# The bias of ScalarE's exps: a constant in the instruction instead of a column in on-chip memory

## The chip, the cores and the metric

The kernel runs on one core of a Trainium2 chip. The metric is the time of one execution on the device, in microseconds (us). The core has a matmul engine (TensorE, PE in the profile; PEld is its weight loads), three engines that work on elements (VectorE is DVE, ScalarE is ACT, GpSimd is POOL) and a queue that only issues DMAs (SyncE, SP). Each works through its own list of instructions in order, and waits on semaphores for the others.

## The reference

Two attention blocks are computed from inputs of their own, and their outputs stand side by side. Each has 2048 rows of 640 numbers in bfloat16, 32 heads of 20.

```python
# A: softmax attention
qkv = (x @ wqkv) -> q, k, v          # 32 heads, 2048 x 20 each
scores = q @ k^T * 20 ** -0.5        # 2048 x 2048 per head
a = (softmax(scores) @ v) @ wo
# B: linear attention
phi(t) = where(t > 0, t + 1, exp(t)) + 1e-6
kv, z = phi(k)^T @ v, sum over s of phi(k)
b = ((phi(q) @ kv) / (phi(q) . z + 1e-6)) @ wo
out = concatenate([a, b])            # 2048 x 1280
```

The large part is block A: 32 heads x 2048 x 2048 scores, each of which needs an exponential.

## The kernel before

**Tiles of A.** A stage `n` is one group of four heads and one block of 512 queries; there are 8 x 4 = 32 of them. Keys are taken 128 at a time. One score matmul (`score`) makes the scores of one head, 128 keys and 512 queries, in one bank of PSUM, the memory into which TensorE writes. It uses 20 rows of the array, so that up to four heads run beside one another. Scores stand with keys on the partitions and queries along the row. The weighted sum of V (`pv_quad`) takes the exponentials as they are; a column of ones in V gives the denominator, by which the result is divided once a stage is complete (`norm`). So a factor that is common to all exponentials drops out.

**Exponentials in two ways.** Most tiles go to ScalarE: `emit_exp` makes one ACTIVATE of a group of three or two tiles in turn (banks 0 to 2, or banks 3 and 4), 1536 or 1024 numbers on each of 128 partitions, and writes bfloat16 into the ring `f_PT`. It computes exp(scale x score + bias), with scale 20 ** -0.5 and bias (42 + 0.000108) ln 2: the factor 2 ** 42 is that of the other way, so that both are on one scale. One or two of the 16 blocks of keys in each stage but one (`ND`) go to VectorE, which forms the exponential in integer and polynomial steps (`d_score`: L1286 once for each tile, then L1297, L1301 and L1305 for two tiles at once) and writes it into `f_PD`.

**The bias column.** `alloc` reserves `f_eb`, 128 partitions of one float32. GpSimd fills it at the start (L1035, in `start_loads`), and each exp of L1251 is given a pointer to it. Block B's exps (`phi`, L1554: 320 or 512 numbers, out of PSUM, into float32) have no bias argument, so the instruction holds the constant 0, and scale 1.

**The loop.** `run` goes over the groups `j`. In each round it writes, for TensorE, the scores of group `j + 1` (`emit_scores`), for ScalarE the exp of group `j`, and then for TensorE products with V and work of the background: projections of Q, K and V, all of block B, and the output projections, whose results VectorE, ScalarE and GpSimd carry on. Scores of group `j + 1` go into the banks that the exp of group `j - 1` reads, so they wait until it is done. Everything else on TensorE that stands ahead of them in its list delays them as well.

**What sets the order.** The lists are written when the kernel is built, by a planner (`_Sched`, `_Clock`) that keeps an assumed time for each engine. It takes 0.062 + 0.4267 n us for an exp of n tiles (L1254) and fills TensorE up to the assumed end of that exp. Where TensorE would have too little to do, it adds matmuls of zeros (`zeros` and `fill`, operands `f_g` and `f_z`) until its sum of assumed work within 3.41 us is at least `FLOOR` = 1.45. `_Sched` writes a wait only where no earlier wait of the engine covers it. At the end a value is read that decides whether a general form of block A is run as well; with these inputs it is not.

Of the kernel before, what the change touches and what calls it, by code (L numbers as in the profile page):

```python
# [5 lines left out]
F32 = mybir.dt.float32  # L6
# [718 lines left out]
LN2 = 0.6931471805599453  # L725
# [74 lines left out]
class _Fast:  # L800
# [53 lines left out]
    def alloc(self):  # L854
        S, NT = self.S, self.NT
        self.KT = self.sb("f_KT", [128, 2, S], BF16)
        self.Qr = self.sb("f_Qr", [128, 4, 512], BF16)
        self.V = self.sb("f_V", [128, NT, N_HEADS, 21], BF16)
        self.xT = self.sb("f_xT", [128, N_DC, S], BF16)
        self.wA = self.sb("f_wA", [128, N_DC, 3 * D_MODEL], BF16)  # L860
        self.wo = self.wA[:, :, 2 * D_MODEL:3 * D_MODEL]
        self.wo7 = self.sb("f_wo7", [128, D_MODEL], BF16)
        self.PT = self.sb("f_PT", [128, self.NPT, 512], BF16)
        self.PD = self.sb("f_PD", [128, self.NPD, 512], BF16)
        self.W = self.sb("f_W", [128, 2, 1024], F32)
        self.PL = self.sb("f_PL", [128, 2, 1024], F32)
        self.T1 = self.sb("f_T1", [128, 512], F32)
        self.Tn = self.sb("f_Tn", [128, 512], BF16)
        self.OTp = self.sb("f_OTp", [128, 512], BF16)
        self.R = self.sb("f_R", [128, 32], F32)  # L870
        self.OTd = self.sb("f_OTd", [128, N_DC, S], BF16)
        self.stage = self.sb("f_st", [128, 4, D_MODEL], BF16)
        self.wBq = self.sb("f_wBq", [128, N_DC, D_MODEL], BF16)
        self.wBkv = self.sb("f_wBkv", [128, N_DC, 2 * D_MODEL], BF16)
        self.woB = self.wBkv[:, :, 0:D_MODEL]
        self.pqT = self.wBkv[:, :, D_MODEL:D_MODEL + 512]
        self.xBt = self.sb("f_xB", [128, 2, N_DC, 512], BF16)
        self.xB = [self.xBt[:, k] for k in range(2)]
        self.kvm = self.sb("f_kvm", [128, N_DC, 21 * N_HEADS], BF16)
        self.kvx = self.sb("f_kvx", [128, 2688 + 10 * 168 + 5 * 168], BF16)  # L880
        self.va = self.kvx[:, 0:2688].rearrange("p (t h j) -> p t h j", t=4, j=21)
        self.kvacc = self.kvx[:, 2688:4368].bitcast(F32).rearrange("p (c n) -> p c n", c=N_DC)
        self.mask = self.kvx[:, 4368:5208].rearrange("p (c n) -> p c n", c=N_DC)
        self.part = self.kvx[:, 0:5120].bitcast(F32).rearrange("p (k n) -> p k n", k=8)
        self.pko = self.sb("f_pk", [128, 4 * D_MODEL], BF16)
        self.pk = self.pko[:].rearrange("p (t n) -> p t n", t=4)
        self.o = self.pko[:, 0:2 * D_MODEL].rearrange("p (t n) -> p t n", t=2)
        self.oT = self.pko[:, 2 * D_MODEL:4 * D_MODEL].rearrange("p (t c m) -> p t c m", t=2, c=N_DC)
        self.ex = self.sb("f_ex", [128, 2, 512], F32)
        self.r1 = self.sb("f_r1", [128, 2, 512], F32)  # L890
        self.rd = self.sb("f_rd", [128, 2, 2, 16], F32)
        self.Z = self.sb("f_z", [128, 128], BF16)
        self.G = self.sb("f_g", [128, 128], BF16)
        self.ebias = self.sb("f_eb", [128, 1], F32)
        self.gmx = self.sb("f_gmx", [128, 2], F32)
        self.ident = self.sb("f_id", [128, 128], BF16)
        self.flag = self.sb("f_flag", [128, 1], I32)
        self.bmx = self.sb("f_bmx", [128, 1], F32)
        self.warm = self.sb("f_warm", [128, 1], F32)
        self.ones = self.sb("f_ones", [128, 1], F32)  # L900
# [115 lines left out]
    def start_loads(self):  # L1016
        sch = self.sch
        awq = self.Aw.rearrange("(c p) n -> p c n", p=128)
        x2 = self.Ax[0]
        xn = self.stage  # L1020
        M = D_MODEL
        for k in range(2):
            sch.dma("sp", lambda e, k=k: e.dma_start(
                xn[:, 2 * k:2 * k + 2, :], x2[256 * k:256 * (k + 1), :].rearrange("(t p) d -> p t d", p=128)),
                writes=tuple(("xn", t) for t in (2 * k, 2 * k + 1)), cost=(0.1, 3.5))
        parts = ((0, 92, ("wq", 0)), (M, M + 92, ("wk", 0)), (2 * M, 2 * M + 160, ("wv", 0)),
                 (M + 92, 2 * M, ("wk", 1)), (92, M, ("wq", 1)), (2 * M + 160, 3 * M, ("wv", 1)))

        def load(q, part):
            a, b, res = part  # L1030
            sch.dma(q, lambda e: e.dma_start(self.wA[:, :, a:b], awq[:, :, a:b]), writes=(res,),
                    cost=(0.5, 5.0 if b - a < 200 else 8.0))
        sch.op("dve", lambda e: e.memset(self.warm[:], 0.0), writes=("warm",))
        sch.op("dve", lambda e: e.memset(self.OTp[:], 1.0), writes=("OTp",), cost=0.3)
        sch.op("pool", lambda e: e.memset(self.ebias[:], (self.OCT + self.EXP_S) * LN2), writes=("ebias",), cost=0.1)  # L1035
        sch.op("act", lambda e: e.activation(self.warm[:], self.warm[:], AF.Exp), writes=("warm",), cost=1.5)
        load("act", parts[0])
        load("act", parts[1])
        load("sp", parts[2])
        for tc in range(1, self.NQC):  # L1040
            for c in range(N_DC):
                sch.dma("sp", lambda e, c=c, tc=tc: e.dma_start_transpose(
                    self.xT[:, c, 512 * tc:512 * (tc + 1)], x2[512 * tc:512 * (tc + 1), 128 * c:128 * (c + 1)]),
                    writes=(("xT", c, tc),), cost=(1.65, 2.0))
        for part in parts[3:]:
            load("sp", part)
# [195 lines left out]
    def emit_exp(self, j):  # L1242
        sch, ps = self.sch, self.ps
        grp = self.groups[j]
        b0 = self.SB[j % 2][0]
        u0 = self.ustart[j]
        s0 = u0 % self.NPT
        n = len(grp)
        assert u0 + n - 1 - self.NPT < 4 * self.pvnext
        scale = float(D_HEAD) ** -0.5  # L1250
        sch.op("act", lambda e: e.activation(self.PT[:, s0:s0 + n, :], ps[:, b0:b0 + n, :], AF.Exp,  # L1251
                                             bias=self.ebias[:, 0:1], scale=scale),
               reads=tuple(("ps", b0 + k) for k in range(n)) + ("ebias",),
               writes=tuple(("PT", s0 + k) for k in range(n)), cost=0.062 + 0.4267 * n)  # L1254

    def d_ready(self, slack):
# [773 lines left out]
```

## Time and profile before

| | us |
|---|---|
| median of 3 runs | 960.22 (959.16 to 965.89) |
| the profiled execution | 961.13 |
| its span, first to last instruction | 959.0 |
| ScalarE busy | 928.6 |
| TensorE busy | 778.2 |
| VectorE busy | 722.0 |
| GpSimd busy | 160.5 |

A row of the groups gives the source line, the engine, the operation, `out<-in` by the names of the tiles, the shapes, the count; then the busy time and the mean duration of one in ns; then how long the engine had been idle just before them, and what ended that. L179 is a helper through which nearly all matmuls are issued, so they are told apart by their operands: `f_Qr,f_KT` are scores, `f_PT,f_V` and `f_PD,f_V` products with V, `f_xT,f_wA` projections of A, `f_wBkv`, `f_xB` and `f_wBq` block B, `f_g,f_z` zeros. The row of clock digits in the slices is the share of its full clock that TensorE was granted, in tenths. In the chain of work each piece has its start, its length and the number of its instructions. In a table of windows each stretch has its length, the busy time and count of each engine (or of one line alone), the granted clock, the share of the DMA engines and GB/s.

### The profile page before, as it was taken

Reading aid. Unit: us, or ns where it says so; the run is one execution under the profiler, and the core shown is the slowest. Engines: PE = TensorE matmul, PEld = TensorE weight load, DVE = VectorE, ACT = ScalarE, POOL = GpSimd, SP = SyncE. Lnnn points to the kernel's source line nnn. Section 1 sums busy time; section 2 is a strip of 40 time slices with the busy share of each in tenths; the row PEclk is TensorE's granted clock in tenths of the full one; section 3 lists DMA queues with packets and bytes.
Section 4 is the critical chain, followed back from the end, with each engine's and each line's share of the span. In section 5 each row is a group of like instructions: output and inputs, shape, how many; then the busy total and the mean of one; then the engine's idle time right before and its main releaser. Section 6 shows DMA issues by size and latency. Waiting matters only on the chain.

```text
span 959.0 us, 24384 instructions
## 1 busy us (share of the span) xinstructions
PE 778.2 (81%) x10963; PEld 244.7 (26%) x10963; DVE 722.0 (75%) x1003; ACT 928.6 (97%) x799; POOL 160.5 (17%) x154
## 2 busy tenths in 40 slices
PE   8877788777778787877788877778887888889986
PEld 3322222222222222322232222212221222223332
DVE  6769576784678888887868787878787788877475
ACT  6999999999999999999989999999999999999996
POOL 3012200010131223221103300041004103200000
PEclk9999979999998999999988899999999999999999
DMA  6900000000001000100040000010001000000001
GB/s 127 251 5 5 4 15 19 4 5 5 16 28 29 5 5 5 32 5 1 5 69 4 2 4 12 19 39 3 21 15 32 12 19 12 1 12 26 33 32 59
DMA packets 45742, 23.93 MB, mean 25 GB/s; under 512 B 33984, under 2 KB 44992, under 8 KB 45632
## 3 DMA queue, kind: packets, MB, share of 16 engines
q1 hardware_dynamic: 44176, 21.92, 9.8%
q8 instruction: 87, 1.43, 0.6%
q10 hardware_dynamic: 1456, 0.40, 0.2%
q14 instruction: 23, 0.19, 0.1%
HBM read 7.31 MB, written 5.24 MB: 13 GB/s over the span
## 4 chain that ended last, share of the span: by engine, by line
ACT 84%; PE 12%; issue 1%; DVE 1%; POOL 0%; DMA 0%; SPq 0%; ACTq 0%
ACT f_PT L1251 81%; PE ps L179 12%; ACT f_ex L1554 2%; DMA f_OTd<-f_OTp 0%; DVE f_PL L1297 0%; SPq L1428 0%; POOL f_pk L1559 0%; PE ps L1064 0%; POOL f_Tn L1409 0%; DVE f_OTp L1416 0%; ACT f_st L1528 0%; DVE f_PD L1305 0%; DVE f_PL L1301 0%; DVE f_kvx L1465 0%; DVE f_V L1178 0%
## 5 line engine op out<-in xcount | busy, mean ns | idle before, releaser
L1251 ACT ACTIVATE f_PT<-ps,f_eb 128x1536 bf16<-128x1536 f32 x739 | 918.3, 1527 | 14.5 <-PE ps L179 14.2
L179 PE MATMUL ps<-f_Qr,f_KT 20*128 20x512 bf16 x2048 | 320.0, 395 | 166.7 <-ACT f_PT L1251 150.8
L179 PE MATMUL ps<-f_g,f_z 32*128 32x512 bf16 (+3 forms) x857 | 227.4, 396 | 0.0
L1286 DVE TENSOR_SCALAR f_W<-ps 128x512 f32<-128x512 f32 x200 | 138.2, 691 | 117.0 <-PE ps L179 113.3
L179 PEld LDWEIGHTS ps<-f_Qr,f_KT 20*128 20x128 bf16 x2048 | 77.7, 91 | 456.6 <-ACT f_PT L1251 425.6
L179 PE MATMUL ps<-f_PT,f_V 128*21 128x512 bf16 x1848 | 189.0, 399 | 1.0 <-ACT f_PT L1251 1.0
L1305 DVE SCALAR_TENSOR_TENSOR f_PD<-f_PL,f_W 128x1024 uint16<-128x1024 f32 x100 | 126.6, 1266 | 0.7
L1301 DVE SCALAR_TENSOR_TENSOR f_PL<-f_W,f_PL 128x1024 f32<-128x1024 uint16 x100 | 126.1, 1262 | 0.9
L1297 DVE SCALAR_TENSOR_TENSOR f_PL<-f_W 128x1024 f32<-128x1024 uint16 x100 | 126.3, 1267 | 0.4
L1409 POOL TENSOR_TENSOR f_Tn<-f_T,f_R 128x320 bf16<-128x320 f32 x31 | 39.2, 1264 | 432.4 <-DVE f_R L1406 432.4
L179 PE MATMUL ps<-f_xT,f_wA 128*32 128x512 bf16 x1280 | 107.4, 406 | 0.0
L1557 POOL TENSOR_SCALAR f_ex<-f_ex 128x320 f32<-128x320 f32 (+1 forms) x52 | 41.3, 795 | 328.1 <-ACT f_ex L1554 328.1
L179 PEld LDWEIGHTS ps<-f_PT,f_V 128*21 128x21 bf16 x1848 | 45.4, 89 | 111.6 <-issue 109.3
L179 PE MATMUL ps<-f_wBkv,f_xB 128*32 128x320 bf16 x1280 | 69.2, 304 | 0.0
L179 PEld LDWEIGHTS ps<-f_g,f_z 32*128 32x128 bf16 (+1 forms) x857 | 53.3, 92 | 7.9 <-issue 7.0
L1559 POOL TENSOR_TENSOR f_pk<-f_ex,f_r 128x320 bf16<-128x320 f32 x32 | 38.4, 1201 | 2.7
L179 PEld LDWEIGHTS ps<-f_xT,f_wA 128*32 128x32 bf16 x1280 | 30.0, 97 | 29.6 <-issue 18.2
L1550 DVE TENSOR_SCALAR f_r<-ps 128x320 f32<-128x320 f32 (+1 forms) x52 | 29.2, 561 | 10.6 <-PE ps L179 10.1
L1554 ACT ACTIVATE f_ex<-ps 128x320 f32<-128x320 f32 (+1 forms) x52 | 36.7, 706 | 0.1
L179 PEld LDWEIGHTS ps<-f_wBkv,f_xB 128*32 128x32 bf16 x1280 | 30.3, 96 | 21.1 <-issue 11.0
L179 PE MATMUL ps<-f_xB,f_wBq 128*32 128x512 bf16 x400 | 34.8, 418 | 0.0
L1399 DVE STREAM_TRANSPOSE f_T<-ps 128x512 f32<-128x512 f32 x32 | 22.8, 713 | 15.7 <-PE ps L179 15.6
(80 smaller groups left out, 504.5 us busy)
## 6 DMA issues: line engine op xcount, KB each, us to landing
out_dram<-f_st SPq DMA_DIRECT2D x31, 160.0 KB
f_OTd<-f_OTp SPq DMA_DIRECT2D x108, 20.0 KB
f_wBkv<-in_B_wqkv_dram SPq DMA_DIRECT2D x1, 1600.0 KB
f_wA<-in_A_wqkv_dram SPq DMA_DIRECT2D x2, 685.0 KB
f_wBq<-in_B_wqkv_dram SPq DMA_DIRECT2D x1, 800.0 KB
f_wA<-in_A_wo_dram SPq DMA_DIRECT2D x1, 800.0 KB
f_wBkv<-in_B_wo_dram SPq DMA_DIRECT2D x1, 800.0 KB
f_st<-in_A_x_dram SPq DMA_DIRECT2D x2, 320.0 KB
```

What stands on the lines that cost most here:

```text
L179: lambda e: e.matmul(out, lhsT, rhs, start=start, stop=stop, tile_position=tp, skip_group_check=sgc),
L1251: sch.op("act", lambda e: e.activation(self.PT[:, s0:s0 + n, :], ps[:, b0:b0 + n, :], AF.Exp, bias=self.ebias[:, 0:1], scale=scale), reads ...
L1286: self.dve(0.69, lambda e: e.tensor_scalar(dst, ps[:, b, :], cs, cb, op0=ALU.mult, op1=ALU.add), reads=(("ps", b),), writes=(("W", x, h),))
L1297: self.dve(1.29, lambda e: e.scalar_tensor_tensor(pl, lo, self.EXP_A, lo, op0=ALU.add, op1=ALU.mult), reads=rw, writes=(("PL", x),), fill= ...
L1301: self.dve(1.29, lambda e: e.scalar_tensor_tensor(pl, lo, self.EXP_B, pl, op0=ALU.add, op1=ALU.mult), reads=rw, writes=(("PL", x),), fill= ...
L1305: self.dve(1.29, lambda e: e.scalar_tensor_tensor(pd, pl, self.EXP_K, w, op0=ALU.mult, op1=ALU.add), reads=rw + (("PL", x),), writes=(("PD ...
L1399: self.dve(0.69, lambda e: e.transpose(T1[:], ps[:, self.PVB, :]), reads=(("ps", self.PVB),), writes=("T1",))
L1409: sch.op("pool", lambda e: e.tensor_tensor(n3[:, :, 0:D_HEAD], t3[:, :, 0:D_HEAD], rb, op=ALU.mult), reads=("T1", ("R", n % 2)), writes=(" ...
L1550: self.dve(0.16 + 0.00104 * n, lambda e: e.tensor_scalar(r1, src, 0.0, 1e-6, op0=ALU.max, op1=ALU.add), reads=(("ps", b),), writes=(("r1", ...
L1554: sch.op("act", lambda e: e.activation(ex, src, AF.Exp), reads=(("ps", b),), writes=(("ex", k),), cost=0.05 + 0.00084 * n)
L1557: sch.op("pool", lambda e: e.tensor_scalar(ex, ex, 1.0, 0.0, op0=ALU.min, op1=ALU.max), writes=(("ex", k),), cost=0.1 + 0.0019 * n)
L1559: self.done[key] = sch.op("pool", lambda e: e.tensor_tensor(dst, ex, r1, op=ALU.add), reads=(("ex", k), ("r1", k)), writes=(res,), cost=0. ...
```

## The change

The column and the instruction that fills it are left out, and the exps are given the number itself. It is the same number in float32. The built instruction of L1251 then has a constant as its bias operand, where it had an address.

```diff
@@ alloc
-        self.ebias = self.sb("f_eb", [128, 1], F32)
@@ start_loads
-        sch.op("pool", lambda e: e.memset(self.ebias[:], (self.OCT + self.EXP_S) * LN2), writes=("ebias",), cost=0.1)
@@ emit_exp
         sch.op("act", lambda e: e.activation(self.PT[:, s0:s0 + n, :], ps[:, b0:b0 + n, :], AF.Exp,
-                                             bias=self.ebias[:, 0:1], scale=scale),
-               reads=tuple(("ps", b0 + k) for k in range(n)) + ("ebias",),
+                                             bias=(self.OCT + self.EXP_S) * LN2, scale=scale),
+               reads=tuple(("ps", b0 + k) for k in range(n)),
                writes=tuple(("PT", s0 + k) for k in range(n)), cost=0.062 + 0.4267 * n)
```

## The prediction

> **What bounds the kernel now.** I read the page's parts 1 and 4 first, for the engine on which the end hangs.
>
> ```profile
> span 959.0 us, 24384 instructions
> PE 778.2 (81%) x10963; PEld 244.7 (26%) x10963; DVE 722.0 (75%) x1003; ACT 928.6 (97%) x799; POOL 160.5 (17%) x154
> PEclk9999979999998999999988899999999999999999
> ACT f_PT L1251 81%; PE ps L179 12%; ACT f_ex L1554 2%; DMA f_OTd<-f_OTp 0%; DVE f_PL L1297 0%; SPq L1428 0%; POOL f_pk L1559 0%; PE ps L1064 0%; POOL f_Tn L1409 0%; DVE f_OTp L1416 0%; ACT f_st L1528 0%; DVE f_PD L1305 0%; DVE f_PL L1301 0%; DVE f_kvx L1465 0%; DVE f_V L1178 0%
> L1251 ACT ACTIVATE f_PT<-ps,f_eb 128x1536 bf16<-128x1536 f32 x739 | 918.3, 1527 | 14.5 <-PE ps L179 14.2
> ```
>
> ScalarE is busy 97% of the span, 918.3 us of it with 739 exps of one line, L1251, and that line holds 81% of the chain that ended last. It stood idle for matmuls 14.2 us in all. The operands say `f_PT<-ps,f_eb`: each of these exps reads the column `f_eb`. This is the instruction that the change touches.
>
> Durations of ScalarE are no use here: back to back, the records overlap (739 x 1.527 us would be 1128 us). The chain of work, in order of time, counts each exp from the end of the one before it, so its pieces give the pace. The groups by form and the timeline say which shapes they hold.
>
> ```profile
> L1251 ACT ACTIVATE f_PT<-ps,f_eb 128x1536 bf16<-128x1536 f32 x370 | 643.8, 1740 | 13.5 <-PE ps L179 13.3
> L1251 ACT ACTIVATE f_PT<-ps,f_eb 128x1024 bf16<-128x1024 f32 x369 | 484.6, 1313 | 0.9 <-PE ps L179 0.9
> ...
> 198.70 0.33 ACT f_ex L1554
> 199.03 41.43 ACT f_PT L1251 x34
> ...
> 51.62 6.31 ACT f_PT L1251 x5
> ...
> 399.04 5.88 ACT f_PT L1251 x5
> ...
> 629.57 0.49 ACT f_ex L1554
> ...
> 198.22 0.81 ACT L1554 ACTIVATE f_ex<-ps 128x320 f32<-128x320 f32 x1
> 629.11 0.95 ACT L1554 ACTIVATE f_ex<-ps 128x512 f32<-128x512 f32 x1
> ```
>
> The exps alternate between 1536 and 1024 elements. Five with three long ones take 6.31 us, five with three short ones 5.88; so one long and one short take 12.19 / 5 = 2.438 us, their difference is 0.43, and they are 1.434 and 1.004 us. The 34 in a row agree: 41.43 / 17 = 2.437 a pair, 1.2185 an exp.
>
> **What the bias costs.** The kernel has exps without a pointer already: L1554, whose bias is a constant 0. One of 320 elements takes 0.33 us on the chain, one of 512 takes 0.49. That is 0.16 / 192 = 0.833 ns an element and a fixed 0.33 - 0.267 = 0.063 us. On that line, 1024 and 1536 elements come to 0.917 and 1.343 us, 2.260 a pair. The pointered pair takes 0.177 more, **0.0885 us an exp**.
>
> L1251 differs from L1554 in three more ways, and each can be priced. It writes bfloat16 and not float32; the two casts at the end do too, from the same float32 banks:
>
> ```profile
> 952.87 0.76 ACT L1528 CAST f_st<-ps 128x320 bf16<-128x320 f32 x2 [3.93 <-PE ps L179]
> L1528 ACT CAST f_st<-ps 128x320 bf16<-128x320 f32 x3 | 1.2, 428 | 4.4 <-PE ps L179 4.4
> ```
>
> The second starts 0.76 - 0.43 = 0.33 us behind the first, just as L1554 does: the type costs nothing. It reads two or three banks, not one; but the excess is 0.087 us with two (1.004 - 0.917) and 0.091 with three (1.434 - 1.343), so a further bank costs 0.004 at most. And it has a scale other than 1, which no row prices alone; that stays, and is why a rival below keeps a chance.
>
> On this the Trainium skill, in "ScalarE: Activation LUTs", section "What ACT_TABLE_LOAD costs", says two things that pull apart: a pointer operand adds about 93 ns to an ACTIVATE, and back-to-back ACTIVATEs overlap by about 93 ns. Read so that the overlap swallows the fetch, the change would bring nothing; the chain above speaks against that reading, since L1251 is 0.0885 us behind the constant-bias line while running back to back. With the page's 93 ns the whole sum would be an estimated 739 x 0.093 = 68.7 us.
>
> **The rest of the change.**
>
> ```profile
> 0.73 0.10 POOL L1035 MEMSET f_eb<- 128x1 f32 x1 [0.29 <-POOLq L2015]
> ```
>
> This memset goes: 0.10 us on POOL near the start, ahead of an iota whose result VectorE needs. The first eight matmuls wait for another memset, VectorE's own, so at most 0.1 us moves; I count nothing. The exps lose a named dependence, but no wait: the built instructions of PE, VectorE, ScalarE and SP stand in the same order, with the same waits at the exps, and POOL has one less. Nothing is added, no DMA is moved, and no engine gets a new instruction.
>
> **How much arrives at the end.** All 739 exps would save 739 x 0.0885 = 65.4 us. That holds only where ScalarE leads. What comes next is PE, and PE has a clock that falls.
>
> ```profile
> core 0: 959.0 us, clock 0.959
> 133.40:143.70 10.30, 8.63 (x7) 0.51 0.13 31
> 512.00:518.80 6.80, 6.14 (x5) 0.54 0.06 14
> 526.00:532.80 6.80, 5.82 (x6) 0.52 0.01 2
> 495.20:502.00 6.80, 4.20 (x4) 0.52 0.52 70
> ACT f_PT L1251 <- PE ps L179: 14.2, 22, 2.2
> PE ps L179 <- ACT f_PT L1251: 151.9, 362, 1.1
> ```
>
> The first row is the core's mean granted clock; the next four are stretches at about half clock, with L1251's busy time and count. At a mean of 0.959 between 1.0 and 0.5, 2 x 0.041 x 959 = 78.6 us are spent at half clock. In the four stretches 22 exps start in 30.7 us, 1.395 us each instead of 1.2185: there PE sets the pace and a shorter exp is worth nothing. 78.6 / 1.395 = 56 exps fall out, and 683 x 0.0885 = **60.4 us** stay. A second count goes by the chain: 81% of 959 us at 1.2185 is 637 exps, worth 56.4 us; it also leaves out what PE works off behind each such stretch. I take 60.4, because the other side pulls as much: the half-clock stretches follow a lull of PE, and lulls get shorter.
>
> ```profile
> sum 54.56, PE 34.89 PEld 10.34 DVE 41.49 ACT 53.97 POOL 13.47; mean PE 2.18 PEld 0.65 DVE 2.59 ACT 3.37 POOL 0.84
> sum 68.20, PE 53.77 PEld 16.72 DVE 54.44 ACT 68.20 POOL 3.15; mean PE 2.69 PEld 0.84 DVE 2.72 ACT 3.41 POOL 0.16
> ```
>
> These are the last lines of two tables of windows of 3.41 us: the 16 windows just ahead of the drops of the clock (PE busy 2.18 us on average) and 20 in a row at full clock, from 550 us on (2.69). ScalarE was busy 3.37 of 3.41 us in the former, so PE's lull is PE waiting for exps. The same matmuls in 1.130 us an exp instead of 1.2185 make 2.18 into 2.35: some of the 16 drops go, not all.
>
> Elsewhere PE has room: it waited 151.9 us for L1251, against 65.4 to be taken away. The tightest stretches and VectorE:
>
> ```profile
> 850.00:900.00 50.00, 45.23 (x710) 16.55 (x710) 34.94 (x61) 49.21 (x42) 1.45 (x2) 0.97 0.06 21
> 900.00:948.00 48.00, 41.68 (x669) 15.71 (x668) 31.20 (x46) 46.85 (x39) 1.58 (x1) 0.96 0.11 39
> DVE f_W L1286 <- PE ps L179: 113.3, 138, 3.3
> ```
>
> From 850 to 948 us PE is idle 98 - 86.9 = 11.1 us, and 81 exps there want 7.2: enough, but nearly used up. VectorE works 722 us, 80% of 900, and waits 113.3 us for scores now. PE is what is late next, then VectorE.
>
> The profiled execution took 961.1 us (span 959.0 and 2.1 around it): 961.1 - 60.4 = 900.7. The median of the runs, 960.2, lies 0.9 below it, so I predict **900 us**.
>
> **Rivals.**
> *The excess is not the pointer's* (the scale, or the overlap that the page tells of): the page of the changed kernel shows the same 2.44 us a pair, 961 us. For it: no exp with a constant bias and this scale has been measured. Against: all else is priced above. Chance 0.03.
>
> *PE and VectorE become the bound more widely.* Then only long unbroken runs of exps gain.
>
> ```profile
> 34.12 17.17 ACT f_PT L1251 x14
> ...
> 932.78 16.17 ACT f_PT L1251 x13
> ```
>
> These are the first and the last of the chain's 23 pieces of ten exps or more; the 23 hold 449 exps: 449 x 0.0885 = 39.7 us, 921 us. For it: the thin margin from 850 us on, and VectorE at 80%. Against: the 151.9 us. Chance 0.15.
>
> *The half-clock stretches go.* Then all exps gain and the 14.2 us of waits go too: 961.1 - 65.4 - 14.2 = 881.5, 881 us. For it: the table of lulls; against: 2.35 us is still under the 2.69 of quiet stretches. Chance 0.17. The Trainium skill, "TensorE: Matmul & The Clock Gate", section "What's actually happening", has it that activity in a window of 3.4 us releases the throttle; the lulls ahead of the drops agree.
>
> *Slower: the clock falls more often.* If the faster exps let PE's work bunch so that lulls recur, each further exp at half clock costs 1.395 - 1.130 = 0.265 us. To end over 1% above the old time, 70 us have to be lost, 264 more exps: 320 of 739, 446 us at half clock against 79 now. At half of the exps it would be 900.7 + 314 x 0.265 = 984 us. Place: the stretch from 495 to 544 us, where such drops already follow one another. Against: denser work is what keeps the clock. Chance 0.02.
>
> **How the numbers follow.** The forecast has 0.63 (890 to 912 on its own). The range goes from the vanished half clock to the gain of long runs alone, 881 to 921. Under 1% (9.6 us) a measurement of this kernel could hardly be told from no change. Faster by over 1%: 0.95 (forecast 0.63, PE 0.15, clock 0.17); same 0.03; slower 0.02.
>
> **What would show it.** In the changed profile: L1251's operands without `f_eb`; chain pieces of 2.26 us a pair; PE's wait for L1251 down from 151.9 to some 90 us; a granted clock of 0.96 to 0.98; ScalarE at about 96%. A pair still at 2.44 us would refute the price; a pair of 2.26 with ScalarE under 93%, idle for PE, would show PE as the bound. Wrong by more than the range it is only if PE's clock behaves otherwise than here.

## The result and the profile after

| | before | after |
|---|---|---|
| median of the runs, us | 963.06 (959.16 to 969.66, 4 runs) | 897.31 (892.96 to 903.53, 4 runs) |
| ratio, with its 95% interval | | 0.9316 (0.9235 to 0.9396) |
| the profiled execution, us | 961.13 | 892.96 |

The change makes the kernel 6.8% faster, 900 us was forecast. Here and below a time is the median of all runs, while a ratio leaves out runs that took over 1.5% longer than the fastest of the same kernel and compares with runs of the kernel before from the same series, so it need not be the quotient of the medians shown. The page of the kernel after, in its parts 1, 2, 4 and 5:

```profile
span 890.8 us, 24383 instructions
PE 754.4 (85%) x10963; PEld 243.1 (27%) x10963; DVE 722.4 (81%) x1003; ACT 863.4 (97%) x799; POOL 164.0 (18%) x153
PEclk9999999999999999999989999999999999999999
...
ACT 82%; PE 10%; DVE 4%; issue 2%; DMA 1%; SPq 0%; POOL 0%; ACTq 0%; DVEq 0%
...
L1249 ACT ACTIVATE f_PT<-ps 128x1536 bf16<-128x1536 f32 x739 | 851.6, 1444 | 10.8 <-PE ps L179 10.1
```

The exps now stand at L1249, and their operands are `f_PT<-ps`: the column is gone. ScalarE was busy 928.6 us and is busy 863.4, 65.2 less; it was idle 959.0 - 928.6 = 30.4 us and is idle 27.4, 3.0 less. Together that is the 68.2 us by which the span is shorter. So the gain is nearly all in the exps' own time. VectorE has exactly the work it had, 722 us, and now has 4% of the chain instead of 1%.

The chain's pieces in order of time give the pace, as before (start, length, instructions):

```profile
48.70 5.86 ACT f_PT L1249 x5
...
102.42 5.44 ACT f_PT L1249 x5
...
183.43 0.33 ACT f_ex L1552
183.76 38.42 ACT f_PT L1249 x34
```

38.42 / 17 = 2.260 us a pair, the very number that the constant-bias line gave: 0.0885 us less for each exp. The waits (us in total, times, the longest) and the core's granted clock:

```profile
PE ps L179 <- ACT f_PT L1249: 107.9, 298, 1.0
DVE f_W L1284 <- PE ps L179: 77.8, 107, 3.3
PEld ps L179 <- DVE f_W L1284: 10.1, 37, 0.9
ACT f_PT L1249 <- PE ps L179: 10.1, 17, 1.9
PEld ps L179 <- DVE f_PD L1303: 6.4, 9, 1.6
```

```profile
core 0: 890.8 us, clock 0.990
```

PE still waits for exps more than for anything else. Its clock rose from 0.959 to 0.990 in this execution (0.968 to 0.990 over the four), and PE's busy time fell by 24 us with the same matmuls, of which fewer ran at half clock.

### The profile page after: what moved, and what is told of

The parts are those of the page before. It is cut to its first block, busy times and chain, and to the rows that moved or that the text cites. A ratio compares the mean times of both kernels' runs of the same rounds, so it can differ in the third digit from the quotient of the medians.

```text
span 890.8 us, 24383 instructions
## 1 busy us (share of the span) xinstructions
PE 754.4 (85%) x10963; PEld 243.1 (27%) x10963; DVE 722.4 (81%) x1003; ACT 863.4 (97%) x799; POOL 164.0 (18%) x153
## 4 chain that ended last, share of the span: by engine, by line
ACT 82%; PE 10%; DVE 4%; issue 2%; DMA 1%; SPq 0%; POOL 0%; ACTq 0%; DVEq 0%
ACT f_PT L1249 79%; PE ps L179 10%; ACT f_ex L1552 3%; DVE f_PD L1303 1%; DVE f_PL L1295 1%; DMA f_OTd<-f_OTp 1%; SPq L1426 0%; DVE f_W L1284 0%; DVE f_PL L1299 0%; DVE f_OTp L1414 0%; DVE f_r L1548 0%; DVE f_T L1397 0%; POOL f_pk L1557 0%; POOL f_Tn L1407 0%; PE ps L1062 0%
## 5 line engine op out<-in xcount | busy, mean ns | idle before, releaser
L1249 ACT ACTIVATE f_PT<-ps 128x1536 bf16<-128x1536 f32 x739 | 851.6, 1444 | 10.8 <-PE ps L179 10.1
L179 PE MATMUL ps<-f_g,f_z 32*128 32x512 bf16 (+3 forms) x857 | 223.0, 386 | 0.0
L179 PE MATMUL ps<-f_PT,f_V 128*21 128x512 bf16 x1848 | 184.3, 388 | 0.9 <-ACT f_PT L1249 0.9
L1303 DVE SCALAR_TENSOR_TENSOR f_PD<-f_PL,f_W 128x1024 uint16<-128x1024 f32 x100 | 128.8, 1288 | 0.7
L1295 DVE SCALAR_TENSOR_TENSOR f_PL<-f_W 128x1024 f32<-128x1024 uint16 x100 | 128.3, 1287 | 0.4
L179 PE MATMUL ps<-f_xT,f_wA 128*32 128x512 bf16 x1280 | 103.1, 390 | 0.0
L1552 ACT ACTIVATE f_ex<-ps 128x320 f32<-128x320 f32 (+1 forms) x52 | 34.8, 670 | 2.3 <-DVE f_r L1548 2.3
L1557 POOL TENSOR_TENSOR f_wBkv<-f_ex,f_r 128x512 bf16<-128x512 f32 x20 | 33.9, 1696 | 1.7
L179 PE MATMUL ps<-f_wA,f_xT 128*32 128x160 bf16 (+1 forms) x640 | 33.1, 301 | 1.1 <-DVE f_V L1176 0.6
```

Source lines behind the costliest of these rows:

```text
L179: lambda e: e.matmul(out, lhsT, rhs, start=start, stop=stop, tile_position=tp, skip_group_check=sgc),
L1295: self.dve(1.29, lambda e: e.scalar_tensor_tensor(pl, lo, self.EXP_A, lo, op0=ALU.add, op1=ALU.mult), reads=rw, writes=(("PL", x),), fill= ...
L1303: self.dve(1.29, lambda e: e.scalar_tensor_tensor(pd, pl, self.EXP_K, w, op0=ALU.mult, op1=ALU.add), reads=rw + (("PL", x),), writes=(("PD ...
L1552: sch.op("act", lambda e: e.activation(ex, src, AF.Exp), reads=(("ps", b),), writes=(("ex", k),), cost=0.05 + 0.00084 * n)
L1557: self.done[key] = sch.op("pool", lambda e: e.tensor_tensor(dst, ex, r1, op=ALU.add), reads=(("ex", k), ("r1", k)), writes=(res,), cost=0. ...
```

## The experiments

**A pointer for the scale instead of the bias.** In `emit_exp` of the kernel before, with a column filled in the place of `f_eb`:

```diff
-   bias=self.ebias[:, 0:1], scale=scale),
+   bias=(self.OCT + self.EXP_S) * LN2, scale=self.scol[:, 0:1]),
```

> The bias is a constant, but the scale of L1251's exps is now a pointer to a column that holds 20 ** -0.5. Theory (any pointer operand costs an ACTIVATE 0.0885 us, whichever it is): the chain shows 1.43 and 1.00 us, 2.44 us a pair, as with the bias pointer, and the time is that of the kernel before, a ratio of 0.99 to 1.01. Rival (the price was the bias's own, for instance its place in the pipeline): 2.26 us a pair and 897 us, a ratio of 0.93.

968.02 us, a ratio to the kernel before of 1.0014 (0.9969 to 1.0058). Its chain:

```profile
50.99 6.30 ACT f_PT L1251 x5
...
108.36 5.88 ACT f_PT L1251 x5
...
199.20 41.41 ACT f_PT L1251 x34
```

41.41 / 17 = 2.436 us a pair. The price belongs to a pointer operand, not to the bias; a scale other than 1 costs nothing as a constant (the kernel after) and the full price as a pointer.

**Both as pointers.**

```diff
-   bias=self.ebias[:, 0:1], scale=scale),
+   bias=self.ebias[:, 0:1], scale=self.scol[:, 0:1]),
```

> Bias and scale are both pointers. Theory (each pointer is fetched by itself, 0.0885 us each): 2.61 us a pair; 739 x 0.0885 = 65 us above the kernel before, some 1025 us, a ratio of 1.06 to 1.08. Rival (two fetches run beside one another, so the price is paid once): 2.44 us a pair, a ratio of 1.00.

1037.13 us, a ratio of 1.0766 (1.071 to 1.0821): inside the ratio that was expected, some 12 us above the time. The chain and the core's clock:

```profile
53.18 6.76 ACT f_PT L1253 x5
...
115.35 6.33 ACT f_PT L1253 x5
```

```profile
core 0: 1029.8 us, clock 0.910
```

A pair takes (6.76 + 6.33) / 5 = 2.618 us, 0.0905 more for each exp than with one pointer. The two prices add up; neither hides the other. 739 x 0.0905 are 66.9 us of the 73 from the kernel before. The remaining 6 us go with a lower clock; that it causes them was not tried by itself.

**A pointer for the long exps only.**

```diff
-   bias=self.ebias[:, 0:1], scale=scale),
+   bias=self.ebias[:, 0:1] if n == 3 else (self.OCT + self.EXP_S) * LN2,
+   scale=scale),
```

> Only the 370 exps of 1536 elements keep the bias pointer; the 369 short ones have the constant. Theory (a fixed price per instruction, and ScalarE leads nearly everywhere): 1.43 us for a long exp, 0.92 for a short one, 2.35 us a pair, and half of the gain, 369 x 0.0885 = 33 us: about 930 us, a ratio of 0.96 to 0.975. Rival (the time gained goes to waits for PE until the whole pair is shorter, or comes from the clock all at once): a ratio off the middle, under 0.95 or over 0.98.

930.08 us, a ratio of 0.9629 (0.9572 to 0.9687). In the chain:

```profile
191.46 39.86 ACT f_PT L1251 x34
```

39.86 / 17 = 2.345 us a pair, halfway between 2.260 and 2.437, and the time is halfway as well (897 and 964). ScalarE's time reaches the end in proportion, so no other engine began to hold the end on the way from one kernel to the other.

**A pointer for block B's exps, in the kernel after.**

```diff
-   e.activation(ex, src, AF.Exp), reads=(("ps", b),), ...
+   e.activation(ex, src, AF.Exp, bias=self.zcol[:, 0:1]), reads=(("ps", b), "zcol"), ...
```

> The kernel after, but the 52 exps of block B get a pointer to a column of zeros for their bias (they had the constant 0). Theory (a fixed price, whatever the size, the destination and its type): on the chain 0.42 us at 320 elements instead of 0.33 and 0.58 at 512 instead of 0.49; 52 x 0.0885 = 4.6 us in all, about 902 us. Rival (the price belongs to long, many-bank or bfloat16 exps): 0.33 and 0.49 us as before.

904.13 us in one run, at a clock of 0.977; the kernel after itself took 892.96 to 903.53, so the time decides nothing here. In its chain:

```profile
188.61 0.41 ACT f_ex L1554
189.02 38.42 ACT f_PT L1251 x34
227.44 0.41 ACT f_ex L1554
```

0.41 us instead of 0.33 for 320 float32 elements, while the large exps beside them keep 2.260 a pair. So the price is about the same for each instruction with a pointer, not a share of its length. An exp of 512 elements shows it as well. This is one in the kernel after, and the same one here:

```profile
485.56 0.49 ACT f_ex L1552
```

```profile
491.27 0.58 ACT f_ex L1554
```

The other pieces of 512 elements here are longer, 0.67 us or more, as most of them are in the kernel after; so the expected 0.58 us rests on one piece.

**Where the clock comes from.** The kernels so far have the same order of instructions on PE, VectorE and ScalarE; only the exps' length differs. From their profiled executions:

| exps | us a pair | granted clock | runs of that kernel, clock |
|---|---|---|---|
| two pointers | 2.618 | 0.910 | 0.896 to 0.910 (4) |
| one pointer (before) | 2.437 | 0.959 | 0.933 to 0.969 (32) |
| one pointer (scale) | 2.436 | 0.948 | 0.938 to 0.962 (7) |
| pointer on the long exps | 2.345 | 0.966 | 0.966 to 0.977 (4) |
| none (after) | 2.260 | 0.990 | 0.968 to 0.990 (4) |

The shorter the exps, the higher the clock: the reading is that the same matmuls in less time keep PE's clock up. What the drops cost shows between the 32 executions of the kernel before: they go from 957.3 us at a clock of 0.963 to 971.0 at 0.933, and a straight line through them gives 0.21 us of time for each us at half clock, between 59 and 130 us of it. Two experiments were meant to move the clock by PE's work instead.

In the first, the planner of the kernel before reckons with exps as long as they are:

```diff
-   writes=..., cost=0.062 + 0.4267 * n)
+   writes=..., cost=0.1505 + 0.4267 * n)
```

> The kernel before, pointer and all, but the planner's price of an exp is raised from 0.062 + 0.4267 n to 0.1505 + 0.4267 n us, what a pointered exp takes; it then writes 1042 zero matmuls for PE instead of 857, and spreads the work behind by longer exps. Theory (the half-clock stretches of before came from lulls, since the plan filled PE for exps shorter than they were): granted clock 0.98 or more instead of 0.959, pairs still 2.44 us, and some 60 us of half clock fewer at 0.19 us each (0.265 / 1.395): 11 us, about 952 us, a ratio of 0.985 to 0.992. Rival (the drops do not hang on this fill): clock near 0.96, a ratio of 1.00.

962.07 us, where the kernel before took 966.43 in the same series: a ratio of 0.9953 (0.9925 to 0.9981), less than half of the gain that was expected. The core's clock and the chain by engine:

```profile
core 0: 960.6 us, clock 0.967
```

```profile
ACT 89%; PE 8%; issue 2%; DVE 1%; ACTq 0%
```

The clock rose to 0.967 in the profile (0.957 to 0.971 over ten runs), not to 0.98. In the same series the kernel before had 0.933 to 0.959. On average that is 0.946 before and 0.965 here, 104 and 68 us at half clock. So a plan that is short of the exps' real length explains about a third of the drops, if the whole difference is put down to it and nothing to the new order.

In the second, the kernel after is left without its zero matmuls; both functions return at once, and the rest is planned anew:

```diff
 def zeros(self, j):
+    return
 def fill(self, limit):
+    return
```

> The kernel after without its zero matmuls (857 of them, which add zeros to sums that are under way); the rest is planned anew. Theory (PE's clock hangs on how densely it is busy, and half clock makes ScalarE wait): granted clock clearly under 0.95, at 0.19 us for each us of half clock 915 us or more. Rival (zeros only take PE's time, which is what is late next): under 897 us.

1018.46 us, a ratio to the kernel before of 1.049 (1.0383 to 1.0597). The page and the waits:

```profile
PE 925.8 (91%) x10106; PEld 254.1 (25%) x10106; DVE 728.0 (71%) x1003; ACT 886.9 (87%) x799; POOL 164.9 (16%) x153
PEclk9957985555586789955895579656998585899579
...
PE 51%; ACT 42%; DVE 4%; issue 1%; POOL 0%; SPq 0%; DMA 0%; ACTq 0%; DVEq 0%
```

```profile
ACT f_PT L1251 <- PE ps L179: 108.4, 168, 5.5
```

```profile
core 0: 1018.6 us, clock 0.747
```

With 857 matmuls fewer PE is busy 171 us longer, because whole stretches run at half clock, and ScalarE waits 108.4 us for scores where it waited 10.1. Here the mechanism of the rival on the slower side is real: with PE's clock low half of the time, the kernel with the short exps is slower than the one with the pointer.

**More tiles for VectorE, and a higher floor.** Both start from the kernel after.

```diff
-    ND = (1, 1, 2, 1, 2, 1, 2, 1, 1, 2, ..., 1, 2, 0, 2)
+    ND = (1, 1, 2, 1, 2, 1, 2, 2, 2, 2, ..., 2, 2, 1, 2)
```

> The kernel after, with four more blocks of keys (16 tiles) given to VectorE: ND is 2 for stages 7, 8 and 28 and 1 for stage 30. If ScalarE still sets the end: 16 tiles of 0.427 us and 6.4 exps' fixed 0.063, 7.2 us less, about 890 us, a ratio to the kernel before of 0.924. Rival (VectorE and PE are already the bound there; VectorE gets 16 x 0.69 + 24 x 1.27 = 41 us more): 897 us or more.

914.94 us, a ratio to the kernel before of 0.9497 (0.9407 to 0.9587).

```diff
-    FLOOR = 1.45
+    FLOOR = 1.55
```

> The kernel after with FLOOR 1.55 instead of 1.45, so 905 zero matmuls instead of 857. If the clock's remaining drops (0.968 to 0.990 from run to run) come from lulls that more zeros fill, the clock is 0.985 or more and the time some 3 us less, about 894 us. Rival (more zeros delay the scores behind them): 900 us or more.

917.09 us, a ratio of 0.9529 (0.9448 to 0.961), at a clock of 0.948 to 0.972 and not 0.985. By the expectations, both rivals would have it: VectorE was the bound, and more zeros delay scores. But both edits have the planner write a new order, and so a control was run that changes next to nothing:

```diff
-   writes=..., cost=0.062 + 0.4267 * n)
+   writes=..., cost=0.064 + 0.4267 * n)
```

> The kernel after, with the planner's fixed price of an exp at 0.064 instead of 0.062 us: a control for planning anew. The assumed pace changes by 0.2%, but the written order does change (820 zero matmuls instead of 857). If the order of after is one of many that are as good, 897 us within 5. If a new plan by itself scatters the time, 905 to 920 us, and then the 915 and 917 us of the kernels with more tiles for VectorE and with FLOOR 1.55 say nothing about those two edits.

913.33 us, a ratio of 0.95 (0.9447 to 0.9553). Its waits and its clock:

```profile
ACT f_PT L1249 <- PE ps L179: 23.7, 25, 5.5
PEld ps L179 <- DVE f_PD L1303: 14.7, 14, 3.7
```

```profile
core 0: 905.8 us, clock 0.967
```

A price of an exp that differs by 0.002 us costs 16 us, nearly as much as the other two edits; the median of the kernel before moved only between 960.22 and 966.43 from series to series. ScalarE waits 23.7 us for scores instead of 10.1, single waits reach 5.5 us, and PE waits for VectorE's exponentials (`f_PD`) 14.7 us instead of 6.4. So the two experiments before it show nothing of their own edits; that more tiles for VectorE do not pay is not shown.

**A plan for longer exps, and a lower floor.** The fixed price of 0.1505 us, now in the kernel after:

```diff
-   writes=..., cost=0.062 + 0.4267 * n)
+   writes=..., cost=0.1505 + 0.4267 * n)
```

> The kernel after, with the planner's fixed price at 0.1505 us, so with the PE order of the pointered kernel with a longer plan (1042 zero matmuls, other work spread over longer exps), while the exps take 0.0885 us less than planned. If PE has room to spare, 900 us or less and a clock of 0.98 or more, since PE is denser than ever. Rival (PE filled for 2.44 us a pair cannot follow 2.26): PE takes the lead, 920 us or more, and ScalarE waits for scores well over 14 us.

908.77 us, a ratio of 0.9428 (0.9382 to 0.9473), between the two expectations, at a clock of 0.966 to 0.976 and not 0.98. Its chain by engine, and ScalarE's wait for scores:

```profile
ACT 65%; DVE 16%; PE 14%; issue 2%; POOL 1%; SPq 0%; DMA 0%; ACTq 0%; DVEq 0%
```

```profile
ACT f_PT L1249 <- PE ps L179: 24.7, 31, 2.3
```

ScalarE still holds most of the chain, so PE with 1042 zero matmuls could nearly follow 2.26 us a pair. It is no slower than the control, and decides no more than that. Then a lower floor in the kernel after:

```diff
-    FLOOR = 1.45
+    FLOOR = 1.35
```

> The kernel after with FLOOR 1.35 (793 zero matmuls instead of 857). If the floor sets the clock: drops more frequent, clock under 0.97, 905 us or more. If it does not at this pace: 897 us or less, and fewer zeros leave PE more room.

901.16 us in one run, at a clock of 0.968. The lower floor lies inside the scatter of new plans, so this decides nothing either. None of these versions beats the kernel after.

## Why the prediction was right

**The price of the pointer** was right: 2.260 us a pair was worked out from the chain pieces of block B's exps, and 2.260 was measured. That the third digit agrees is luck. The pieces are given to 0.01 us, and 0.33 and 0.49, each off by 0.005, would give anything from 2.17 to 2.35 us a pair, so 0.04 to 0.13 us an exp. A slope that the prediction did not use bears it out: L1251's own, 0.43 us for 512 elements, is 0.84 ns an element. The three other differences between the lines were priced at nothing, and the kernel after agrees, since with scale, type and banks unchanged only the operand differs. The rival that the excess is not the pointer's fell, and with it the reading of the Trainium skill ("ScalarE: Activation LUTs", section "What ACT_TABLE_LOAD costs") by which the overlap of ACTIVATEs swallows the fetch. The other number of that section of the Trainium skill, 93 ns for each pointer operand, stands close to 0.0885 us for the first pointer, 0.0905 for the second and 0.08 at 320 elements.

**How much arrives at the end** was 60.4 us in the prediction and 62.9 to 65.8 between medians (960.22 or 963.06 to 897.31), 68.2 between the profiled executions. Of these 68.2, ScalarE's busy time gave 65.2, which is what all 739 exps were to give, and its idle time 3.0.

The term that was mis-sized is the half clock. The prediction took off 5.0 us for 56 exps that would only wait longer for PE, and it set shorter lulls against no more than the 4.0 us by which its second count lay lower. By that, ScalarE's waits for scores would have grown by 5.0 us; they fell by 4.1, from 14.2 to 10.1. It had said that some of the 16 drops go, with a clock of 0.96 to 0.98; the profiled execution had 0.990, the others 0.986, 0.986 and 0.968. At 0.959 and 0.990 that is 2 x 0.041 x 959.0 = 79 and 2 x 0.010 x 890.8 = 18 us at half clock, 61 us fewer. At 0.21 us each this would be some 13 us, but that line was drawn between 59 and 130 us, and 18 lies outside.

ScalarE's waits, taken one by one from the timelines with the clock beside them, give less. Of the 14.2 us before, 8.8 stand in or right behind a stretch at half clock; of the 10.1 us after, 2.6. The wait of the first exp (1.9 us) and those in one stretch of background matmuls (3.0 us, around 495 us before and 457 us after) are the same in both. The rest, at full clock, rose from 0.5 to 2.6 us. So the drops that went gave 6.2 us, and new waits at full clock took 2.1 of them back.

VectorE has come nearer: PE waits for its `f_W` and `f_PD` 16.5 us after, against 5.8 in the kernel before, whose two rows are these, and VectorE's share of the chain rose to 4%.

```profile
PEld ps L179 <- DVE f_W L1286: 3.9, 16, 0.5
...
PEld ps L179 <- DVE f_PD L1305: 1.9, 4, 1.0
```

Little of that reaches ScalarE. By the chain, 0.9 us of its new waits for scores stand right behind `f_PD` (0.6 at 484.54 and 0.3 at 826.93 us), and block B's exps waited 2.3 us for VectorE's `f_r`, where it was 0.1 before.

That 900 lies so near to 897 is in part luck: the sum fell 7.8 us short of the execution for which it was made, and the other executions of the kernel after ran at a lower clock than the profiled one.

**The price of half clock** was put at 0.265 / 1.395 = 0.19 us for each us, with the short exps. The same working with the exps of the kernel before gives (1.395 - 1.2185) / 1.395 = 0.13, where its executions give 0.21; the kernel without zero matmuls lies (1020.69 - 892.96) / (515 - 18) = 0.26 above the kernel after, the new plan included. So each further us at half clock costs more than the prediction took. Why it does, and why the waits within the profiled executions give less (6.2 us for 61), stays open.

**PE's wait for exps** was to fall to some 90 us and fell to 107.9. The step that was off is the same one: fewer drops made PE's own work 24 us shorter, so it waits longer, 151.9 - 68.2 + 24 = 107.7.

**The rivals.** That PE and VectorE become the bound more widely was refuted by the time, 897 and not 921 us, and by the half-way kernel: half of the pointers gave half of the time. That the half-clock stretches go came partly true. The lulls ahead of the drops were not idle, though: PE was busy 1.84 to 2.62 of 3.41 us in them, and eight of the 20 quiet windows lay within that and kept the clock, such as this one (the first number behind the length is PE's busy time, the third from the end the clock):

```profile
570.46:573.87 3.41, 2.22 (x39) 0.75 (x35) 3.22 (x6) 3.41 (x4) 0.93 (x1) 1.00 0.00 0
```

So less work of PE goes with a drop, but where the limit lies is not shown. The slower side needed the clock low for 446 us; the kernel without zero matmuls, at 2 x 0.253 x 1018.6 = 515 us, is slower than before, so the mechanism holds, and the change did not set it off.

## What to carry to other kernels

Where one engine's instructions fill the chain back to back, take the price of an operand from the pace of a similar instruction that lacks it, not from durations, which overlap; here a constant in place of a pointer was worth 0.0885 us each, 739 times. Before a second edit is judged in a kernel whose order a planner writes, run a control that makes it plan anew: here that alone moved the time by 16 us. And when the leading engine gets faster, look at what its pace does to TensorE's clock.

## What was not expected

The plan is very sensitive: with the planner's price of an exp at 0.064, 0.1505 or 0.062 us the same kernel takes 913, 909 or 897 us, and why the order of the last is the better one stays open. And the clock is worth more than was predicted, 0.21 to 0.26 us for each further us at half clock. The group of zero matmuls in the kernel after (count, busy us, mean ns):

```profile
L179 PE MATMUL ps<-f_g,f_z 32*128 32x512 bf16 (+3 forms) x857 | 223.0, 386 | 0.0
```

These 223 us of work on nothing, and the plan that goes with them, separate 897 us from 1018.
